# A fused FFT filter and two mixture-of-experts layers on one core: the order of an expert's blocks, prefetch hints for far branches, and the engine that makes the weights' low parts

## The chip, the cores and the metric

One NeuronCore of a Trainium2 chip runs the whole program in one launch. The metric is the device time of one execution in microseconds; lower is better. Engines: PE (TensorE, whose weight loads are listed as PEld), DVE (VectorE), ACT (ScalarE), POOL (GpSimd) and SP (SyncE, which issues most of the DMAs).

## The reference, cut to what matters

```python
X = rfft(x, axis=1)                      # x: (8, 3072, 256)
y = irfft(X * (filt_r + 1j * filt_i))    # a filter per channel
x = y.reshape(24576, 256)
# first layer: every token, 8 experts, top 1
e_idx = argmax(x @ w_gate)
out[e_idx == e] = gate_w * sigmoid(x @ w_output_gate)[e] * (relu(x[e_idx == e] @ w1[e]) @ w2[e])
# second layer: at most 768 tokens an expert, in the order of the tokens; all other rows are 0
```

The number of tokens of an expert is known at run time only, and so is which tokens the second layer takes.

## The kernel before

Products that need more than one pass's precision are split: a high part, rounded by ACT, and a low part, the value less its high part. Each product is then three matmuls (high by high, high by low, low by high). This holds for activations (`xt_h`, `xt_l`, `h_h`, `h_l`) and for the weights (`w_0h`, `w_0l`, ...), whose two sets serve even and odd experts.

**Stages of the profiled execution.** Up to 340 us: the FFT of eight batches and the gate of the first layer, which scatters each token's row into its expert's region of `xs`. The first 86 of 192 token tiles (11008 tokens) are treated first, and what is left is skipped at the end if the second layer's places are full by then (`k.full`, L1864), as they are here. From 340 to 416 us: expert 0's first four blocks in `one_round`, under a guess that they exist (`early`, L712), with the gate's last work beside them. From 416 to 968 us: the rest of the first layer in `Moe.moe1`. Then the second layer in `Moe.moe2`, 24 blocks of 256 rows, until 1307 us.

**An expert in moe1.** Its rows are cut into plain blocks of 256 rows and a last block of 256 (narrow) or 384 rows (wide), which is taken from the end of its region (`cut_blocks`). In program order: block 0, which always runs; then up to seven more plain blocks, each inside the If of the one before it (`nb > j`, L1211), so that an expert with four plain blocks leaves the chain by one far branch over the bodies that are left; then the last block, an If on `wide` with one arm for each size (L911). Here experts 0 to 7 have 4, 5, 5, 4, 4, 5, 5 and 3 plain blocks; experts 3, 4, 5 and 7 have wide last blocks.

**A block (`block1`).** Layer 1 in four pairs (`l1_pair`, 12 matmuls each; ACT makes `h_h` and DVE `h_l`), then `prep` of the next block's rows (four transposes on PE, `xt_h` by ACT, `xt_l` by DVE), then layer 2 for two tiles of 128 rows (24 matmuls each), each followed by an indirect DMA of the rows to `x2tok` on POOL. PE takes all of this in program order. DVE also makes 16 logits of the block before (L1040, a product with a row of `w2gb` and its sum), each block's ending in indirect DMAs to `lgtok`.

**Loads.** SP loads the rows of block j + 1 while block j runs (`load_x`; buffers a0 to a2 for j > 0, b0 and b1 for block 0). Where block j + 1 doesn't exist, `k.ahead` clamps the address to the last real block, and `prep` turns rows that nobody uses. At an expert's start SP loads block 0 of the next expert, block 1 of this one, and the last block's rows (`load_last`). Block 0 turns the rows of block 1 right after its layer 1, and the rows of the last block within its layer 2.

**Weights.** `extra` puts four steps `next_w` into block 0 of each expert: for one quarter of the next expert's weights each, ACT makes the high part, POOL the low part (L810; DVE for the first two experts' weights), and POOL then issues the load of the quarter after next. `moe2` does the same at each expert's block 0.

**Order.** PE, ACT, DVE and SP run in the order in which the program was written; POOL's order is the scheduler's. At the end of an If each engine that skipped its body brings its semaphores up to what the body would have made of them. For POOL's DMA queues that is a wait for the DMAs in flight and then the instruction INC_SWDGE_SEM.

Of the kernel before, what the change touches and what calls it, by code (L numbers as in the profile page):

```python
# [25 lines left out]
EARLY = 4  # L26
# [437 lines left out]
def one_round(k, r, cap):  # L464
# [46 lines left out]
    for bi, b in enumerate(batches):  # L511
# [68 lines left out]
        for q in range(NQ + 2):  # L580
# [17 lines left out]
            if nb is None and q in (4, 6, 8, 10):  # L598
                moe.split_w(0, (q - 4) // 2, nc.vector)
            if nb is None and q == 8 and len(batches) > 1:  # L600
# [4 lines left out]
                with tc.If(early > 0):  # L605
                    moe.load_x(0, 0, True)
        j0, j1 = span[b]
# [54 lines left out]
    def aheads():  # L662
# [21 lines left out]
        )  # L684
        nc.vector.tensor_copy(k.ahead, k.aheadf)

    work = [gate.chain_a2, gate.chain_b, counts, pads, aheads, lambda: cut_blocks(k)]
# [20 lines left out]

    if early is None:
        late()  # L710
    else:
        with tc.If(early > 0) as c:  # L712
            for j in range(1, EARLY):
                moe.load_x(0, j, True)
            weights()
            run(last[0])
            moe.prep(*moe.rows(0, 0))
            moe.head(0, [(0, 1)], last[1:])
            nc.sync.dma_start(out=moe.w2gb, in_=k.a["w2gb"])
            beside = [work[:0], work[:0], work[:2], work[2:4], work[4:5], work[5:]]  # L720
            moe.head(1, [(0, 2)], [lambda f=f: run(*f) for f in beside], True)
            for j in range(2, EARLY - 1):
                moe.head(j, [(0, j + 1)])
            ahead()
            moe.load_x(0, EARLY)
            moe.head(EARLY - 1, [(0, None), (0, EARLY)])
        with c.Else():
            late()
# [5 lines left out]
class Moe:  # L734
# [15 lines left out]
    def alloc(self, p, px):  # L750
# [14 lines left out]
        k.pm = p.tile([128, 3, 8], F32, name="pm")  # L765
# [34 lines left out]
    def split_w(self, g, part, eng=None):  # L800
        nc = self.nc
        eng = eng or nc.gpsimd
        s = g % 2
        if part < 2:
            raw, hi, lo = self.raw1[:, part, :], self.w1[s][0][:, part, :], self.w1[s][1][:, part, :]
        else:
            i = slice(4 * (part - 2), 4 * (part - 2) + 4)
            raw, hi, lo = self.raw2[:, i, :], self.w2[s][0][:, i, :], self.w2[s][1][:, i, :]
        nc.scalar.copy(hi, raw)
        eng.tensor_tensor(out=lo, in0=raw, in1=hi.bitcast(F32), op=ALU.subtract)  # L810
# [63 lines left out]
    def load_x(self, e, j, free=False):  # L874
# [3 lines left out]
        if j > 0 and not free:  # L878
# [4 lines left out]
                max_val=r0,  # L883
# [22 lines left out]
    def last_block(self, e, wide):  # L906
# [3 lines left out]
        nxt = [] if final else [self.rows(e + 1, 0)]  # L910
        with self.tc.If(wide > 0) as c:  # L911
            self.block_wide(s, nxt, final)
        with c.Else():
            xt = [v[:, :, :256] for v in self.xtf]
            self.block1(s, self.xbf[:, :2, :], xt, 3, True, [], nxt, (), final)

    def block_wide(self, s, nxt, final):
# [23 lines left out]
        for rows, x in nxt:  # L941
            self.prep(rows, x)
# [150 lines left out]
    def block1(  # L1093
# [20 lines left out]
        for q in range(4):  # L1114
# [21 lines left out]
        for t in range(2):  # L1136
# [5 lines left out]
            for f in mid[2 + t : 3 + t]:  # L1142
                f()
        for f in side:
            f()
# [17 lines left out]
    def extra(self, e):  # L1163

        n = self.k.last_g
        eng = self.nc.vector if e == 0 else None
        if e + 1 > n:
            return []
        return [lambda q=q: self.next_w(e + 1, n, q, eng) for q in range(4)]
# [8 lines left out]
    def head_late(self, nb, n):  # L1178
# [5 lines left out]
        for j in range(1, n):  # L1184
            with self.tc.If(nb > j):
                self.load_x(0, j + 1)
                self.head(j, [(0, j + 1)])

    def moe1(self, nb0, n0):
# [4 lines left out]
        for e in range(E):  # L1194
# [3 lines left out]
            if e == 1:  # L1198
                nc.sync.dma_start(out=k.iota, in_=k.a["c_iota"])
                nc.sync.dma_start(out=k.jp1, in_=k.a["c_jp1"])  # L1200
            if e == 0:
                nb = nb0
            else:
                nb = nc.values_load(k.plain[0:1, e : e + 1], min_val=0, max_val=nxb)
                self.load_x(e, 1)
# [4 lines left out]
            wide = nc.values_load(k.wide[0:1, e : e + 1], min_val=0, max_val=1)  # L1210
            with ExitStack() as deep:  # L1211
                for j in range(n0 if e == 0 else 1, JU):
                    deep.enter_context(tc.If(nb > j))
                    nxt = []
                    if j + 1 < JU:
                        self.load_x(e, j + 1)
                        nxt = [self.rows(e, j + 1)]
                    self.block1(s, *self.bufs(e, j), 1 + j % 2, True, [], nxt)
# [422 lines left out]
    def moe2(self, n0, n1, plan=None):  # L1641
# [11 lines left out]
        for n in range(n0, n1):  # L1653
# [4 lines left out]
            if b == 0 and e + 1 < E:  # L1658
                mid = [lambda q=q: self.next_w(e + 9, 15, q) for q in range(4)]
# [8 lines left out]
            if b == min(2, nblk - 1):  # L1668
                now, rest = now + rest, []
            for q in range(4):  # L1670
                if n > 0:
                    self.l1_pair(s, self.xt, q)
                if q == 1:
# [16 lines left out]
            for t in range(2):  # L1690
# [18 lines left out]
                go(5 + t)  # L1709
            run(now[split[1] :])  # L1710
# [9 lines left out]
def tile_kernel(ctx: ExitStack, tc, a, out, cap, dbg=None):  # L1720
# [96 lines left out]
    with tc.manual_schedule(engines={ET.PE, ET.Activation, ET.DVE, ET.SP}):  # L1817
        for r in range(len(ROUNDS)):
# [3 lines left out]
            def body():  # L1822
# [4 lines left out]
                with es:  # L1827
                    if last:
                        table(moe.p, r)
                    if last:  # L1830
# [7 lines left out]
                        for q in range(4):  # L1838
                            moe.next_w(8, 9, q)
                        moe.q = es.enter_context(tc.tile_pool(name=f"q{r + 1}", bufs=1))  # L1840
                        moe.go("HPDGKLMBX0123")
                    else:
                        n = len(moe.seq) // E
                        moe.go(LEAD[0])
                        moe.first.close()
                        moe.q = es.enter_context(tc.tile_pool(name=f"q{r + 1}", bufs=1))
                        moe.guess = False
                        pre = nc.values_load(k.known[0:1, 0:1], min_val=0, max_val=1)
                        with tc.If(pre > 0) as c:
                            xg = dict(moe.xg)  # L1850
                            moe.moe2(0, n, BESIDE)
                        with c.Else():
                            moe.xg = xg
                            moe.xg.clear()
                            moe.go(LEAD[1])
                            moe.moe2(0, n)
# [18 lines left out]
LEAD = ("KTUVXLWlMB01ax23yse", "bHPDGeomhctfKLsMBrX0123")  # L1875
# [17 lines left out]
def cut_consts():  # L1893
# [3 lines left out]
    return np.stack([2 * least + 1, 2 * least + 3, least])  # L1897
# [63 lines left out]
```

## Time and profile before

| | |
|---|---|
| median of 3 executions | 1326.87 us (1322.34 to 1327.99) |
| the profiled execution | 1321.05 us, its span 1319.3 us |
| PE busy | 1207.2 us, 92% of the span |
| DVE busy | 872.0 us, 66% |
| POOL busy | 557.2 us, 42% |
| mean granted clock of PE | 0.961 |

The span runs from the first to the last instruction of the profiled execution. A group's idle time names the engine and line whose semaphore ended most of it; "issue" stands for time in which the engine waited for nothing that the profile shows, such as a branch of its own sequencer. An engine's name with a q is its sequencer.

### The profile page before, as it was taken

The numbers are of one execution on the slowest core, as the hardware profiler recorded it, in microseconds if no ns is written. First come the engines' busy times: TensorE is split into PE (matmuls) and PEld (weight loads), VectorE is DVE, ScalarE is ACT, GpSimd is POOL, SyncE is SP. The second block draws the span as 40 slices with busy tenths as digits, with TensorE's granted clock in tenths as the row PEclk, the third lists the DMA queues.
The fourth block names the chain that finished last, engine by engine and source line by source line (L and its number), as shares of the span: only waits on it lengthen the run. The fifth ranks groups of instructions, "written<-read, shape, count | busy, mean of one in ns | idle before, by whom it ended". The sixth has DMA issues, their size and how long they took to land. (4 is left out here: it accounts for less than half of the span.)

```text
span 1319.3 us, 25824 instructions
## 1 busy us (share of the span) xinstructions
PE 1207.2 (92%) x9338; PEld 1172.9 (89%) x9338; DVE 872.0 (66%) x2800; ACT 490.8 (37%) x872; POOL 557.2 (42%) x508
## 2 busy tenths in 40 slices
PE   6999999999885998989998899998997899999996
PEld 6899999989885998889898889988887899999996
DVE  3857676678473875867868688786857755555541
ACT  4363443633421422424233243332323344444431
POOL 0000160446262542634445273452635567676731
PEclk9999999999897999999999899998998999999998
DMA  9343280634563321513224051320512233333210
GB/s 259 123 139 115 63 276 1 204 128 137 185 178 103 108 80 31 165 44 126 70 67 141 27 159 51 117 89 28 157 41 79 66 106 112 97 99 105 71 46 22
DMA packets 85469, 138.95 MB, mean 105 GB/s; under 512 B 13463, under 2 KB 61339, under 8 KB 84889
## 3 DMA queue, kind: packets, MB, share of 16 engines
q1 hardware_dynamic: 61113, 71.07, 17.9%
q0 software_dynamic: 24144, 65.31, 15.5%
q8 instruction: 102, 1.67, 0.5%
q14 instruction: 110, 0.90, 0.2%
HBM read 78.02 MB, written 58.90 MB: 104 GB/s over the span
## 5 line engine op out<-in xcount | busy, mean ns | idle before, releaser
L827 DVE SCALAR_TENSOR_TENSOR h_l<-ps,h_h 128x512 fp32r<-128x512 f32 x252 | 173.4, 689 | 216.0 <-ACT h_h L826 214.4
L1040 DVE SCALAR_TENSOR_TENSOR junk<-x,w2gb 128x256 f32<-128x256 f32 x640 | 283.4, 494 | 0.0
L826 ACT ACTIVATE h_h<-ps 128x512 fp32r<-128x512 f32 x252 | 149.6, 598 | 211.9 <-PE ps L823 202.3
L1020 POOL DMA_INDIRECT lgtok<-lg,wtok x80 | 78.2, 978 | 254.3 <-DVE junk L1040 237.4
L400 POOL DMA_INDIRECT xs<-y,sli x86 | 87.8, 1021 | 214.9 <-DVE tt L234 115.4
L839 PE MATMUL ps<-w_0h,h_l 128*128 128x256 f32 x552 | 160.4, 291 | 17.0 <-DVE h_l L827 16.7
L839 PE MATMUL ps<-w_1h,h_l 128*128 128x256 f32 x552 | 159.9, 290 | 13.2 <-DVE h_l L827 13.1
L837 PE MATMUL ps<-w_0h,h_h 128*128 128x256 f32 x552 | 162.4, 294 | 0.0
L837 PE MATMUL ps<-w_1h,h_h 128*128 128x256 f32 x552 | 161.3, 292 | 0.0
L838 PE MATMUL ps<-w_0l,h_h 128*128 128x256 f32 x552 | 158.4, 287 | 0.0
L838 PE MATMUL ps<-w_1l,h_h 128*128 128x256 f32 x552 | 158.1, 286 | 0.0
L821 PE MATMUL ps<-xt_h,w_0h 128*128 128x256 f32 x480 | 137.4, 286 | 0.7 <-ACT xt_h L871 0.7
L822 PE MATMUL ps<-xt_l,w_0h 128*128 128x256 f32 x480 | 136.4, 284 | 0.2 <-DVE xt_l L872 0.2
L823 PE MATMUL ps<-xt_h,w_0l 128*128 128x256 f32 x480 | 136.3, 284 | 0.0
L821 PE MATMUL ps<-xt_h,w_1h 128*128 128x256 f32 x464 | 128.9, 278 | 1.6 <-ACT xt_h L871 1.6
L822 PE MATMUL ps<-xt_l,w_1h 128*128 128x256 f32 x464 | 128.8, 278 | 0.0
L823 PE MATMUL ps<-xt_h,w_1l 128*128 128x256 f32 x464 | 128.7, 277 | 0.0
L839 PEld LDWEIGHTS ps<-w_0h,h_l 128*128 128x128 f32 x552 | 107.9, 196 | 20.4 <-DVE h_l L827 20.4
L839 PEld LDWEIGHTS ps<-w_1h,h_l 128*128 128x128 f32 x552 | 107.8, 195 | 16.1 <-DVE h_l L827 15.8
L838 PEld LDWEIGHTS ps<-w_0l,h_h 128*128 128x128 f32 x552 | 108.2, 196 | 0.0
L837 PEld LDWEIGHTS ps<-w_0h,h_h 128*128 128x128 f32 x552 | 108.1, 196 | 0.0
L837 PEld LDWEIGHTS ps<-w_1h,h_h 128*128 128x128 f32 x552 | 107.9, 195 | 0.0
(288 smaller groups left out, 3058.1 us busy)
## 6 DMA issues: line engine op xcount, KB each, us to landing
out<-padrow SPq DMA_DIRECT2D x48, 512.0 KB, 6.4
raw<-v POOLq DMA_DIRECT2D x32, 512.0 KB, 4.2
raw<-w POOLq DMA_DIRECT2D x24, 512.0 KB, 4.4
xin<-x SPq DMA_DIRECT2D x40, 240.0 KB, 3.0
xb_a<-xs SPq DMA_DIRECT2D x35, 258.0 KB, 2.9
raw<-w SPq DMA_DIRECT2D x8, 512.0 KB, 5.9
f<-f SPq DMA_DIRECT2D x13, 256.0 KB, 4.6
xs<-padrow SPq DMA_DIRECT2D x8, 387.0 KB, 10.5
```

Source lines behind the costliest of these rows:

```text
L400: i = nc.gpsimd.indirect_dma_start(out=k.xs, out_offset=bass.IndirectOffsetOnAxis(ap=self.sli[:, j : j + 1], axis=0), in_=self.y[:, self.j ...
L821: nc.tensor.matmul(o, lhsT=wh[:, c, sl], rhs=xh[:, c, :], start=c == 0, stop=False)
L822: nc.tensor.matmul(o, lhsT=wh[:, c, sl], rhs=xl[:, c, :], start=False, stop=False)
L823: nc.tensor.matmul(o, lhsT=wl[:, c, sl], rhs=xh[:, c, :], start=False, stop=c == 1)
L826: nc.scalar.activation(hh, ps, AF.Relu)
L827: nc.vector.scalar_tensor_tensor(out=hl, in0=ps, scalar=0.0, in1=hh.bitcast(F32), op0=ALU.max, op1=ALU.subtract)
L837: nc.tensor.matmul(ps, lhsT=hh[:, f, sl], rhs=wh[:, f, :], start=f == 0, stop=False)
L838: nc.tensor.matmul(ps, lhsT=hh[:, f, sl], rhs=wl[:, f, :], start=False, stop=False)
L839: nc.tensor.matmul(ps, lhsT=hl[:, f, sl], rhs=wh[:, f, :], start=False, stop=f == 7)
L1020: i = nc.gpsimd.indirect_dma_start(out=k.lgtok, out_offset=bass.IndirectOffsetOnAxis(ap=tok, axis=0), in_=lg, in_offset=None, bounds_check ...
L1040: self.nc.vector.scalar_tensor_tensor(out=self.junk[:, n % 2, :], in0=x2, scalar=1.0, in1=self.w2gb[:, e, :], op0=ALU.mult, op1=ALU.mult, ...
```

## The change

Five things change.

1. In moe1 the last block of experts 0 to 6 comes directly after block 0 (after the four guessed blocks for expert 0), ahead of the chain of Ifs. Where block j + 1 of an expert doesn't exist, `k.ahead` now gives the start of the next expert's region (`beyond`, `jump`, `k.pend`), so the last plain block turns the rows of the next expert's block 0. The last block no longer does.
2. `mark_branch_hint_location` puts a prefetch hint for a labelled branch into PE's instruction stream, with the value that the branch will have: for `wide` ahead of block 0 (experts 1 to 6), for `nb > j + 1` ahead of block j and in both arms of the last block, for `late`, `known` and `rest`. Expert 0's `wide` gets none.
3. The likely arms of `late` and `known` become the Else arms, so that they end without a branch over the other arm.
4. The weights' low parts are made by DVE everywhere. The step of each quarter is cut in two: the high part in one place, the low part and the load one place later. The places move from the middle of layer 1 to its end, and a fifth comes after layer 2.
5. `cut_blocks` runs before `aheads`, which has four more DVE instructions on 8x8 elements; one more stands in `cut_blocks`.

```diff
+    STT(out=k.pend, in0=k.cntf, scalar=256.0, in1=k.pm[:, 3, :], op0=ALU.mult, op1=ALU.add)
...
+                tc.mark_branch_hint_location("late", 1 - early, [mybir.EngineType.PE])
...
+            in0=k.j256.unsqueeze(1).to_broadcast(b3),
+            in1=k.pend.unsqueeze(2).to_broadcast(b3),
+            op=ALU.is_ge,
...
+        nxt = k.pm[:, 4, :].unsqueeze(2).to_broadcast(b3)
+        nc.vector.tensor_tensor(out=moe.jump, in0=nxt, in1=k.aheadf, op=ALU.subtract)
+        nc.vector.tensor_tensor(out=moe.jump, in0=moe.jump, in1=beyond, op=ALU.mult)
+        nc.vector.tensor_tensor(out=k.aheadf, in0=k.aheadf, in1=moe.jump, op=ALU.add)
...
-    work = [gate.chain_a2, gate.chain_b, counts, pads, aheads, lambda: cut_blocks(k)]
+    work = [gate.chain_a2, gate.chain_b, counts, pads, lambda: cut_blocks(k), aheads]
...
-        with tc.If(early > 0) as c:
...
+        with tc.If(early < 1, label="late") as c:
+            late()
         with c.Else():
-            late()
+            soon()
...
-    def next_w(self, g, n, part, eng=None):
-        self.split_w(g, part, eng)
-        if g + 1 <= n:
-            self.load_w(g + 1, part, self.nc.gpsimd)
+    def next_w(self, g, n):
+        def step(i):
+            if i > 0:
+                self.split_lo(g, i - 1)
+                if g + 1 <= n:
+                    self.load_w(g + 1, i - 1, self.nc.gpsimd)
+            if i < 4:
+                self.split_hi(g, i)
+        return [lambda i=i: step(i) for i in range(5)]
...
+    def split_lo(self, g, part):
+        raw, hi, lo = self.parts(g, part)
+        self.nc.vector.tensor_tensor(out=lo, in0=raw, in1=hi.bitcast(F32), op=ALU.subtract)
...
+    def hint(self, name, value=0):
+        label = f"{name}{self.k.rname}"
+        self.tc.mark_branch_hint_location(label, value, [mybir.EngineType.PE])
+    def more(self, nb, e, j):
+        self.hint(f"n{e}_{j}_", (nb - j + 63) >> 6)
...
-        nxt = [] if final else [self.rows(e + 1, 0)]
-        with self.tc.If(wide > 0) as c:
-            self.block_wide(s, nxt, final)
+        with self.tc.If(wide > 0, label=f"w{e}_{self.k.rname}") as c:
+            tell()
+            self.block_wide(s, final)
         with c.Else():
+            tell()
...
-            if q == 1:
-                for f in mid[:1]:
-                    f()
         for rows, x in nxt[1:] or nxt:
             self.prep(rows, x)
+        for f in mid[:1]:
+            f()
...
+        for f in mid[4:]:
+            f()
...
+                if final:
+                    self.more(nb, e, 1)
+                else:
+                    self.hint(f"w{e}_", wide)
                 self.load_x(e, 1)
                 self.load_last(e)
                 nxt = [self.rows(e, None), self.rows(e, 1)]
                 zero_out(k, ZFFT + (48 - ZFFT) * e // (E - 1))
                 self.block1(s, *self.bufs(e, 0), 0, True, self.extra(e), nxt)
-            wide = nc.values_load(k.wide[0:1, e : e + 1], min_val=0, max_val=1)
+            first = n0 if e == 0 else 1
+            if not final:
+                self.last_block(e, wide, lambda: self.more(nb, e, first))
             with ExitStack() as deep:
-                for j in range(n0 if e == 0 else 1, JU):
-                    deep.enter_context(tc.If(nb > j))
-                    nxt = []
+                for j in range(first, JU):
+                    deep.enter_context(tc.If(nb > j, label=f"n{e}_{j}_{k.rname}"))
                     if j + 1 < JU:
+                        self.more(nb, e, j + 1)
                         self.load_x(e, j + 1)
                         nxt = [self.rows(e, j + 1)]
...
-            if e + 1 == E and self.guess:
-                self.moe2_steps(0)
-            self.last_block(e, wide)
+            if final:
+                if self.guess:
+                    self.moe2_steps(0)
+                self.last_block(e, wide)
...
+                        pre = nc.values_load(k.known[0:1, 0:1], min_val=0, max_val=1)
+                        tc.mark_branch_hint_location("known", 1 - pre, [mybir.EngineType.PE])
+                        moe.go(LEAD[1])
...
-                        with tc.If(pre > 0) as c:
+                        with tc.If(pre < 1, label="known") as c:
...
-                with tc.If(k.fr < 1):
+                with tc.If(k.fr < 1, label="rest"):
```

## Rows read from the trace of the kernel before

**Rows 1.** The page: engines, with busy us, share of the span and instructions.
```profile
PE 1207.2 (92%) x9338; PEld 1172.9 (89%) x9338; DVE 872.0 (66%) x2800; ACT 490.8 (37%) x872; POOL 557.2 (42%) x508
```

**Rows 2.** Windows: start:end, length, busy us and instructions per engine, clock, DMA share, GB/s.
```profile
416.00:968.00 552.00, 495.13 (x3914) 488.47 (x3914) 413.40 (x1556) 181.32 (x323) 247.99 (x217) 0.95 0.29 89
968.00:1052.00 84.00, 70.29 (x514) 67.53 (x514) 55.60 (x162) 26.22 (x59) 40.65 (x35) 0.88 0.22 67
1052.00:1307.00 255.00, 253.13 (x2244) 251.83 (x2241) 130.01 (x393) 110.01 (x208) 156.44 (x126) 1.00 0.27 85
```

**Rows 3.** Waits of PE, 420 to 968 us: who for whom, us in total, times, longest.
```profile
PE ps L821 <- issue: 25.3, 4, 10.2
PE ps L839 <- DVE h_l L827: 22.4, 16, 2.6
```

**Rows 4.** Windows after an exit, after a wait for DVE, and of one plain block.
```profile
510.90:514.30 3.40, 3.36 (x16) 3.39 (x17) 0.17 (x1) 0.30 (x1) 0.00 (x0) 0.51 0.28 82
...
548.70:551.90 3.20, 3.18 (x15) 3.18 (x16) 3.20 (x16) 0.47 (x1) 1.37 (x2) 0.50 0.59 165
...
480.15:491.81 11.66, 11.66 (x103) 11.66 (x102) 9.13 (x40) 3.82 (x7) 3.97 (x5) 1.00 0.27 71
```

**Rows 5.** Timelines (start, us, engine, line), DVE and POOL beside PE, expert 2.
```profile
545.03 2.67 DVE L1040 SCALAR_TENSOR_TENSOR junk<-x,w2gb 128x256 f32<-128x256 f32 x1
...
547.64 0.41 DVE L1040 SCALAR_TENSOR_TENSOR junk<-x,w2gb 128x256 f32<-128x256 f32 x1
...
545.05 2.37 POOL L810 TENSOR_TENSOR w_1l<-raw,w_1h 128x1024 fp32r<-128x1024 f32 x1
...
548.72 0.58 PE L839 MATMUL ps<-w_0h,h_l 128*128 128x256 f32 x1 [2.58 <-DVE h_l L827]
```

**Rows 6.** Line L810, whole span: ns min/median/max, first and last start.
```profile
L810 POOL TENSOR_TENSOR w_0l<-raw,w_0h x28: 2362/2419/2645, 444.1 to 1219.1; 128x1024 fp32r<-128x1024 f32 x28
...
L810 DVE TENSOR_TENSOR w_0l<-raw,w_0h x4: 1224/1224/1300, 325.1 to 334.0; 128x1024 fp32r<-128x1024 f32 x4
```

**Rows 7.** Branch lines, whole span: count, ns min/median/max, first and last start.
```profile
L1211 DVEq COMPARE_BRANCH  x39: 43/47/67, 417.5 to 969.9; - x39
L1211 PEldq COMPARE_BRANCH  x39: 65/70/4252, 418.4 to 969.4; - x39
...
L1211 POOLq INC_SWDGE_SEM  x8: 621/1336/2254, 422.4 to 972.5; - x8
...
L911 PEldq COMPARE_BRANCH  x12: 85/296/3244, 422.8 to 991.7; - x12
...
L712 PEldq COMPARE_BRANCH  x2: 73/1832/3590, 336.0 to 413.8; - x2
...
L1849 PEldq COMPARE_BRANCH  x2: 73/1914/3755, 1003.9 to 1050.1; - x2
```

**Rows 8.** Expert 1's exit, next work of PE and DVE, PE's branch, SP's next load and landing.
```profile
510.94 0.52 PE L821 MATMUL ps<-xt_fh,w_1h 128*128 128x256 f32 x1 [5.18 <-issue]
...
511.52 0.17 DVE L1111 COPY wtok<-ptok 128x2 int32<-128x2 int32 x1 [6.34 <-DMA lgtok<-lg,wtok]
...
L1211 PEldq COMPARE_BRANCH  x2: 192/1844/3497, 503.5 to 507.2; - x2
...
512.11 0.38 SPq L886 DMA_DIRECT2D xb_a<-xs  x1
...
DMA to landing us min/median/max: 2.7/2.7/2.7
```

**Rows 9.** Groups of PE at L865, 416 to 968 us: busy us, mean ns, idle before.
```profile
L865 PE MATMUL ps<-ident,xb_a 128*128 128x128 f32 x124 | 18.6, 272 | 0.0
```

**Rows 10.** Line L1864, the last branch: PE's and POOL's sequencers.
```profile
L1864 PEldq COMPARE_BRANCH  x1: 3797/3797/3797, 1304.8 to 1304.8; - x1
```

**Rows 11.** Waits of PE, 960 to 1060 us.
```profile
PE ps L839 <- DVE h_l L827: 4.0, 2, 3.0
PE ps L1450 <- DVE tg L1338: 4.0, 3, 3.4
```

More of the change, by code (lines that the diff above doesn't have):

```diff
@@ L707, in late, with soon @@
         moe.head_late(nb, EARLY)
+    def soon():
+        for j in range(1, EARLY):
+            moe.load_x(0, j, True)
+        weights()
+        run(last[0])
+        moe.prep(*moe.rows(0, 0))
+        moe.head(0, [(0, 1)], last[1:])
+        nc.sync.dma_start(out=moe.w2gb, in_=k.a["w2gb"])
+        beside = [work[:0], work[:0], work[:2], work[2:4], work[4:5], work[5:]]
+        moe.head(1, [(0, 2)], [lambda f=f: run(*f) for f in beside], True)
+        for j in range(2, EARLY - 1):
+            moe.head(j, [(0, j + 1)])
+        ahead()
+        moe.load_x(0, EARLY)
+        moe.head(EARLY - 1, [(0, None), (0, EARLY)])
     if early is None:
@@ L711, in one_round @@
     else:
-        with tc.If(early > 0) as c:
[L713 to L726, printed above, removed]
+        with tc.If(early < 1, label="late") as c:
+            late()
         with c.Else():
-            late()
+            soon()
     np = nc.values_load(k.plain[0:1, 0:1], min_val=0, max_val=k.R // 256)
@@ L764, in alloc @@
         )
-        k.pm = p.tile([128, 3, 8], F32, name="pm")
+        k.pm = p.tile([128, 5, 8], F32, name="pm")
+        k.pend = p.tile([128, 8], F32, name="pend")
+        self.beyond, self.jump = (p.tile([128, 8, 8], F32, name=n) for n in ("beyond", "jump"))
         nc.sync.dma_start(out=k.pm, in_=k.a["c_pm"])
@@ L792, in load_w, with parts, split_hi, split_w @@
             )
[L794 to L802 removed]
+    def next_w(self, g, n):
[7 more added lines that the diff above has]
+        return [lambda i=i: step(i) for i in range(5)]
+    def parts(self, g, part):
         s = g % 2
         if part < 2:
[L805 to L810, printed above, removed]
+            return [t[:, part, :] for t in (self.raw1, *self.w1[s])]
+        i = slice(4 * (part - 2), 4 * (part - 2) + 4)
+        return [t[:, i, :] for t in (self.raw2, *self.w2[s])]
+    def split_hi(self, g, part):
+        raw, hi, _ = self.parts(g, part)
+        self.nc.scalar.copy(hi, raw)
+    def split_lo(self, g, part):
+        raw, hi, lo = self.parts(g, part)
+        self.nc.vector.tensor_tensor(out=lo, in0=raw, in1=hi.bitcast(F32), op=ALU.subtract)
+    def split_w(self, g, part):
+        self.split_hi(g, part)
+        self.split_lo(g, part)
     def l1_pair(self, s, xt, q):
@@ L1165, in extra @@
         n = self.k.last_g
[L1166 to L1169, printed above, removed]
+        return self.next_w(e + 1, n) if e + 1 <= n else []
     def head(self, j, nxt, side=(), pe_tail=False):
@@ L1187, in head_late @@
                 self.head(j, [(0, j + 1)])
+        self.load_x(0, n)
+        self.prep(*self.rows(0, n))
     def moe1(self, nb0, n0):
@@ L1658, in moe2 @@
             if b == 0 and e + 1 < E:
-                mid = [lambda q=q: self.next_w(e + 9, 15, q) for q in range(4)]
+                mid = self.next_w(e + 9, 15)
                 if not plan:
@@ L1669, in moe2 @@
                 now, rest = now + rest, []
+            if self.k.rname == "r0" and n + 1 == len(seq):
+                full = nc.values_load(
+                    k.full[0:1, 0:1], engines=(mybir.EngineType.PE,), min_val=0, max_val=1
+                )
+                self.tc.mark_branch_hint_location("rest", 1 - full, [mybir.EngineType.PE])
             for q in range(4):
@@ L1709, in moe2 @@
                 go(5 + t)
+            run(mid[4:])
             run(now[split[1] :])
@@ L1837, in body @@
                             moe.load_w(8, q)
-                        for q in range(4):
-                            moe.next_w(8, 9, q)
+                        for f in moe.next_w(8, 9):
+                            f()
                         moe.q = es.enter_context(tc.tile_pool(name=f"q{r + 1}", bufs=1))
@@ L1896, in cut_consts @@
     least = np.array([EARLY] + [1] * (E - 1))
-    return np.stack([2 * least + 1, 2 * least + 3, least])
+    far = np.where(np.arange(E) == E - 1, 2.0**20, 0.0)
+    nxt = rows_per_expert() * np.minimum(np.arange(E) + 1, E - 1)
+    return np.stack([2 * least + 1, 2 * least + 3, least, far, nxt])
 def misc_consts(cap):
```

37 lines of the change are left out of this document (23 added, 14 removed).

## Prediction

> **What bounds the kernel now.** I read the page first: PE is busy for 92% of the span, DVE for 66% [rows 1]. So time is won where PE stands still or runs at a lower clock, and the windows by stage say where. In the second layer from 1052 us on PE is busy for 253.1 of 255.0 us at full clock: nothing is to be had there but matmuls [rows 2]. In the first layer (416 to 968 us) PE is idle for 552.0 - 495.1 = 56.9 us and its mean clock is 0.95 [rows 2]. The list of PE's waits in that stage splits the idle time: 25.3 us in 4 waits for nothing but its own sequencer, at the exits into a narrow last block; 22.4 us in 16 waits for `h_l` of DVE [rows 3]; the other 9 us stand at the exits into wide blocks.
>
> The clock adds to both. [...]
>
> **Why PE waits for DVE.** The timelines of both engines beside POOL's show it. A logit's product takes DVE 0.41 us, but one that meets POOL's low part took 2.67 us and ended with POOL's 2.37 us instruction; `h_l` stands behind it, and PE waited 2.58 us for it [rows 5]. The kernel has 56 such low parts on POOL, 2.4 us each; DVE makes one in 1.22 us [rows 6].
>
> **Low parts on DVE.** Removed in the first layer: the 22.4 us, and, at an estimate for six of the seven experts, 1.6 us of slow clock, 10 us: 32 us. Added on DVE per expert: 4 x 1.22 = 4.9 us; removed there: each of four POOL instructions can hold a DVE instruction for up to 2.3 us (2.67 - 0.41), so DVE comes out about even. DVE is busy for 9.1 of a plain block's 11.66 us [rows 4], 2.5 us short of PE. In block 0 it now needs 9.1 + 4.9 = 14.0 us and a little for the last block's rows, against some 13 us of PE. What is late next is thus the `h_l` of the block behind block 0: PE needs the first of them 5.5 us after that block's start, so the lag of 1 to 2 us is mostly covered. Without that cover each expert would pay the lag. I charge 0.6 us an expert, 4 us in all; bounds 0 and 30 us (a rival, below). Net: -28 us. POOL loses nothing by its place: its loads of the next weights wait for DVE instead of itself, and have an expert's length to land.
>
> **Exits of the chain.** PE's far branches took up to 4.25 us (3.50 at expert 1's exit) [rows 7, 8]. PE's sequencer runs ahead: that branch began at 503.5 us, 2.3 us before the last matmul ended (510.94 - 5.18 = 505.76) [rows 8]. A hinted branch that takes what a fall-through takes (0.07 us [rows 7]) would end before PE runs dry. But another wait starts at the same point. POOL closes the skipped bodies' semaphores only when its DMAs have landed, with an INC_SWDGE_SEM of 0.6 to 2.3 us [rows 7]; DVE's next copy came 5.8 us after PE's last matmul, and SP's load of the next expert's block 1 (buffer a1, whose earlier readers are in the chain) was issued at 512.11, 6.35 us after it, to land 2.7 us later: 9.05 us [rows 8]. Before, the last block lay between the exit and block 0, and hid that. Now block 0 follows at once. Its layer 1 is half of a block's matmuls: a block less its four transposes (0.6 us: 124 transposes in 18.6 us [rows 9]) is 11.06, half is 5.5 us. Then PE wants block 1's rows: it is idle for 9.05 - 5.5 = 3.6 us an exit, however fast the branch. With 1.7 to 3 us of slow clock behind it an exit costs 5.3 to 6.6 us, say 5.9; experts 0 to 6 make 41 us. SP's load of the last block's rows is queued behind that load and lands after it; PE wants them one layer 2 tile later, so I price it at 0 (its cover is that tile, some 2.8 us). Before, these exits cost 56.9 - 22.4 = 34.5 us of idle time and some 12 us of clock (seven exits at 1.7), 46 us.
>
> **Entries.** Expert 0's arm of `late` ended with a branch of 3.59 us and went on into two more [rows 7]; the three made the 10.2 us wait [rows 3]. Now only the unhinted one over the wide arm is left (at most 3.2 us [rows 7], less 2.3 of run-ahead), with some slow clock and a wait of DVE behind it: 4 us. Exits and entry after: 45 us. Net: -1 us.
>
> **Transposes.** For experts 0 to 6 four transposes turned rows that nobody used, and the last block turned the next expert's: one of the two goes, 7 x 0.6 = -4 us, on PE's path.
>
> **Expert 7, `known`, `rest`.** Expert 7's exit keeps its place, so the hint helps it: -1 us of its share. `known` jumps over the other arm in 3.76 us [rows 7]; less the 2.3 us of run-ahead, -1 us. The last branch (`rest`) takes 3.8 us from 1304.8 us [rows 10] but POOL's end of the DMAs comes later: 0; bounds 0 and -1 us.
>
> **Start of the second layer.** PE waits there 4.0 us for `h_l` and 4.0 us for the gates' casts [rows 11], with a clock of 0.88 over the stage [rows 2]; both stand behind POOL's low parts. DVE gets four low parts of 1.22 us in the same stretch, which take back about 5 us. -4 us; bounds 0 and -10 us.
>
> **At nothing.** The hints' register arithmetic on PE hides in the 2.3 us of run-ahead, at exits in the 3.6 us wait; the five new DVE instructions on 8x8 elements are nearest to the 0.17 us copy [rows 8], some 1 us once, under the load wait of that stretch; loads that now carry the next expert's rows are as many as before.
>
> **The sum.** -28 - 1 - 4 - 2 - 4 = -39 us, against the profiled execution's 1321.05: 1282. The median of the three runs lies 5.8 us above that execution, so I forecast 1287 us as the median.
>
> **Rivals.**
> 1. *The load is not held back* (15%): if SP's load after the exit need not wait for POOL's increments, an exit costs one to two us and little clock, 2.8 instead of 5.9: 7 x 3.1 = 22 us better, 1265 us. For it: the hints would then pay in full. Against it: buffer a1 is read only by bodies in the chain, and SP's load waited at that point at the exit shown [rows 8].
> 2. *DVE becomes the bound* (14%): block 0's DVE work, started late by POOL's increments (its copy came 5.8 us after the exit [rows 8]), pushes `h_l` past PE's need by 2.5 us, and the slow clock adds 1.6: 7 x 4.1 = 29 us, 1316 us. It decides once DVE's lag passes PE's 5.5 us of layer 1. Against it: 2.5 us of DVE slack in each later block [rows 4].
> 3. *The hints do nothing* (10%): the change would not do what it says at far branches. The exits' branches, at 3.5 us less 2.3, end before the load does, so only the three narrow entries of experts 1, 2 and 6 (3.2 - 2.3 = 0.9 us and 1.7 of clock each) and `known` pay: 8 us, 1295 us. [...]
> 4. *A hint pushes out the code that comes next* (6%): slower. In the first layer 23 of the 39 branches (39 less two for each of 8 exits) are the not-taken ones of bodies that run, at 0.07 us now [rows 7]. If a hint's fetch displaced the fall-through code, each would pay about 3.5 - 2.3 = 1.2 us and 1.7 us of clock: 23 x 2.9 = 67 us, 1354 us. It turns the gain into a loss from 39 / 23 = 1.7 us a branch. Against it: the hint carries the branch's true value.
>
> **How the numbers follow.** The forecast's own case has 55%, from 1274 to 1302 us. The range of 8 in 10 reaches to rival 1 below and near rival 2 above: 1264 to 1314 us. The measurement can tell about 0.5% of this kernel from no change, 6.6 us. Faster by more: the forecast, rivals 1 and 3 and most of rival 2, 0.87. Within: the rest of rival 2 and some of rival 4's weaker forms, 0.07. Slower: rival 4, 0.06.
>
> **What would show it.** No DVE product of the logits over 1 us, and PE's waits for `h_l` in the first layer at 5 us or less instead of 22: the low parts. PE's branches of the chain under 0.3 us: the hints. PE's transposes waiting for `xb_a` some 3 us, seven times, with SP's load 6 us after the exit: the exits. 28 transposes less at L865 in the stage: the transposes. The forecast is wrong if exits are free of that wait, if `h_l` stays late behind DVE's low parts, or if bodies that run begin with a fetch.

## The result, and the profile after

The changed kernel takes 1265.7 us (median of 4 runs, 1258.9 to 1268.1) beside 1326.1 us for the kernel before (1322.3 to 1328.0): a ratio of 0.954, 95% interval 0.950 to 0.958. The forecast was 1287 us, the range 1264 to 1314: the sign and the range held, but the gain is 60 us where 39 were forecast. The profiled execution took 1263.8 us, its span 1262.0; before, 1321.05 and 1319.3.

The page of the changed kernel (engines with busy us, share and instructions; then TensorE's granted clock in 40 slices), and its windows by stage, which answer [rows 1, 2]:

```profile
PE 1187.2 (94%) x9310; PEld 1154.3 (91%) x9310; DVE 860.4 (68%) x2854; ACT 489.3 (39%) x865; POOL 419.0 (33%) x452
...
PEclk9999999999999999999999999999978999999998
```
```profile
416.00:914.00 498.00, 473.69 (x3915) 468.00 (x3913) 393.98 (x1582) 181.89 (x320) 181.85 (x189) 1.00 0.31 98
914.00:996.00 82.00, 72.31 (x514) 69.36 (x514) 50.91 (x171) 25.99 (x60) 30.24 (x32) 0.85 0.24 74
996.00:1250.00 254.00, 252.71 (x2240) 251.82 (x2240) 143.01 (x412) 108.94 (x207) 95.59 (x102) 1.00 0.26 85
```

The first layer's stage shrank from 552 to 498 us; the start of the second layer gained 2 us, the rest 1. The stage's granted clock is 1.00 where it was 0.95 [rows 2]. PE's waits in it (us, times, longest) answer [rows 3]:

```profile
PE ps L898 <- DMA xb_a<-xs: 10.9, 7, 2.8
PE ps L854 <- ACTq L1261: 8.0, 6, 1.4
PE ps L854 <- issue: 2.3, 1, 2.3
PE ps L854 <- ACT x L1180: 1.2, 1, 1.2
PE ps L872 <- DVE h_l L860: 0.9, 3, 0.3
```

The 22.4 us for `h_l` are 0.9, the 25.3 us for the sequencer 2.3. In their place stand a wait of 1.1 to 2.3 us at each exit, mostly for ScalarE's sequencer (8.0 us in six waits), which takes its own branch at L1261 (38 and 50 ns at expert 2), and one for block 1's rows. Expert 2's exit (start, us, engine, line), then the window behind its second wait (PE, PEld, DVE, ACT, POOL busy, granted clock):

```profile
580.27 0.28 PE L872 MATMUL ps<-w_0h,h_l 128*128 128x256 f32 x1
581.95 0.38 PE L854 MATMUL ps<-xt_h,w_1h 128*128 128x256 f32 x1 [1.41 <-ACTq L1261]
```
```profile
587.70 0.37 SPq L919 DMA_DIRECT2D xb_a<-xs  x1
```
```profile
590.57 0.66 PE L898 MATMUL ps<-ident,xb_a 128*128 128x128 f32 x4 [2.77 <-DMA xb_a<-xs]
```
```profile
590.60:594.00 3.40, 3.40 (x29) 3.40 (x30) 2.07 (x10) 2.48 (x3) 0.42 (x1) 1.00 0.98 302
```

PE's last matmul ends at 580.55, SP issues the load 7.15 us later and PE gets the rows 2.8 us after that, as forecast (6.35 and 2.7). Until then SP had waited for the DMAs to `x2tok` that read that buffer (us, times, longest):

```profile
SPq L919 <- DMA x2tok<-x,xb_a: 21.4, 1, 21.4
```

But two waits of PE, of 1.4 and 2.8 us, with half a block of work between them stand where the forecast had one of 3.6, and in this profile no lower clock follows.

VectorE's products of the logits, for [rows 5] (ns min/median/max; none reaches 0.5 us):

```profile
L1081 DVE SCALAR_TENSOR_TENSOR junk<-x,w2gb x640: 404/416/493, 390.5 to 912.5; 128x256 f32<-128x256 f32 x160
```

The branches and transposes, for [rows 7, 10] and [rows 9] (L952 chooses the wide or narrow last block, L1261 ends the bodies, L1912 is `known`; first of the kernel after, then the next-expert rows of the kernel before):

```profile
L1261 PEldq COMPARE_BRANCH  x39: 65/70/1463, 428.5 to 913.8; - x39
...
L952 PEldq COMPARE_BRANCH  x12: 65/308/3112, 418.1 to 939.6; - x12
...
L1912 PEldq COMPARE_BRANCH  x1: 374/374/374, 951.6 to 951.6; - x1
...
L898 PE MATMUL ps<-ident,xb_a 128*128 128x128 f32 x124 | 19.0, 275 | 10.9 <-DMA xb_a<-xs 10.9
```
```profile
L865 PE MATMUL ps<-ident,xb_b 128*128 128x128 f32 x28 | 4.2, 272 | 0.0
```

Those 28 transposes are the ones that went: 9338 matmuls became 9310.

### The profile page after: what moved, and what is told of

The parts are those of the page before. It is cut to its first block, busy times and chain, and to the rows that moved or that the text cites. A ratio compares the mean times of both kernels' runs of the same rounds, so it can differ in the third digit from the quotient of the medians.

```text
span 1262.0 us, 25769 instructions
## 1 busy us (share of the span) xinstructions
PE 1187.2 (94%) x9310; PEld 1154.3 (91%) x9310; DVE 860.4 (68%) x2854; ACT 489.3 (39%) x865; POOL 419.0 (33%) x452
## 5 line engine op out<-in xcount | busy, mean ns | idle before, releaser
L1081 DVE SCALAR_TENSOR_TENSOR junk<-x,w2gb 128x256 f32<-128x256 f32 x640 | 235.5, 420 | 0.0
L872 PE MATMUL ps<-w_1h,h_l 128*128 128x256 f32 x552 | 156.4, 283 | 0.6 <-DVE h_l L860 0.6
L871 PEld LDWEIGHTS ps<-w_1l,h_h 128*128 128x128 f32 x552 | 105.8, 192 | 0.0
```

The lines of the kernel that those rows point to most:

```text
L871: nc.tensor.matmul(ps, lhsT=hh[:, f, sl], rhs=wl[:, f, :], start=False, stop=False)
L872: nc.tensor.matmul(ps, lhsT=hl[:, f, sl], rhs=wh[:, f, :], start=False, stop=f == 7)
L1081: self.nc.vector.scalar_tensor_tensor(out=self.junk[:, n % 2, :], in0=x2, scalar=1.0, in1=self.w2gb[:, e, :], op0=ALU.mult, op1=ALU.mult, ...
```

## The experiments

Twelve runs follow, of nine kernels, on three chips. On one chip the kernel before takes 1390.7 us (last section); the table has the runs of the others: the first layer's stage of each profile, from the start of PE's branch at the end of the head to the start of its exit branch at expert 7. Idle is the stage less the union of PE's matmuls and weight loads; "half clock" is half of PE's busy time inside stretches at a granted clock of 0.50. Both are worked out from the traces.

| kernel | median us | before, beside it | stage us | idle | half clock |
|---|---|---|---|---|---|
| before | 1326.1 | | 552.0 | 56.7 | 22.4 |
| low parts on VectorE only (b_lo) | 1292.7 | 1324.6 | 522.3 | 37.3 | 14.5 |
| hints only (b_hints) | 1310.7 | 1324.6 | 538.2 | 45.7 | 19.8 |
| low parts and hints (b_lo_hints_2) | 1271.6 | 1323.7 | 505.3 | 26.8 | 7.9 |
| all but VectorE (a_lo_pool) | 1312.8 | 1324.6 | 535.9 | 48.9 | 15.1 |
| all but the hints (a_no_hints) | 1269.8 | 1324.6 | 497.8 | 24.6 | 4.9 |
| all: the changed kernel | 1265.7 | 1326.1 | 493.3 | 23.8 | 0.0 |
| the same again (after_2) | 1264.0 | 1323.7 | 495.8 | 23.6 | 3.4 |
| all, rows loaded twice (a_delay_2) | 1286.4 | 1323.7 | 520.0 | 38.6 | 16.1 |
| all, rows in own buffers (a_free_2) | 1253.2 | 1323.7 | 481.9 | 13.4 | 0.0 |

### One part alone: VectorE's low parts

```
-        eng.tensor_tensor(out=lo, in0=raw, in1=hi.bitcast(F32), op=ALU.subtract)
+        self.nc.vector.tensor_tensor(out=lo, in0=raw, in1=hi.bitcast(F32), op=ALU.subtract)
```
with the five new places in the block, and nothing else of the change.

> The kernel before with one part of the change: VectorE makes the low parts, at the new places; the blocks' order, the branches and the hints stay as before. Before stands at 1326. Theory A (two leaks that add up: the waits on h_l while GpSimd and VectorE share work, and the exits): the h_l waits between 420 and 968 us fall from 22.4 us to about 1, the half-clock stretches that followed six of the seven 2.6 us waits (3.4 us each, worth 1.7 us each) go, some 4 us of transposes' and copies' waits go, and the exits keep their 24 us and their own half-clock stretches: 1326 - 21 - 10 = about 1293 to 1297. Rival B (the clock falls only where both leaks come close together, so that it returns only once both are gone): only the waits go, 1303 to 1307, with eight or more half-clock stretches left in that stage. Rival C (VectorE becomes the bound of block 0, as the prediction's second rival had it): the waits return in block 0 under another releaser and the time is 1310 or more.

Measured: 1292.7 us, ratio 0.977 (0.971 to 0.982), 31.9 us less. Theory A. The waits:

```profile
PE ps L835 <- issue: 14.8, 3, 5.1
PE ps L835 <- DVE wtok L1125: 10.5, 1, 10.5
PE ps L943 <- issue: 5.4, 2, 4.9
PE ps L853 <- DVE h_l L841: 2.2, 7, 0.3
```

The `h_l` waits fell from 22.4 to 2.2 us, so VectorE did not become the bound (rival 2, theory C). What remains are the exits and expert 0's entry (10.5), and in or just behind each of these waits a half-clock stretch begins, also where the wait was 1.9 to 2.2 us.

### One part alone: the hints

```
-        deep.enter_context(tc.If(nb > j))
+        deep.enter_context(tc.If(nb > j, label=f"n{e}_{j}_{k.rname}"))
...
+        self.more(nb, e, j + 1)          # a hint ahead of each body
```

> The kernel before with one part of the change: the chain's and the last block's branches have a label, and a body names the coming exit ahead of time; order of blocks and GpSimd's low parts stay as before. Theory A (the hint itself takes the jump's 3.4 us off TensorE's queue): the exit jump falls to about 0.4 us; the exits of experts 1, 2 and 6, which make a second far jump of 2.7 to 3.2 us, go from 5 us of idle time to about 1.5 if the second jump can still start ahead of TensorE's drain, the others from 1.8 to 1.3: 3 x 3.5 + 3 x 0.5 = 12 us, and half of the 27 us of half-clock stretches behind exits goes with it at most (13 us): 1301 to 1315. Rival B (the exits are held by what is not the jump, by the other engines' catch-up and the load's landing): the jump falls to 0.4 us, idle time stays within 4 us of before, and the time is 1321 to 1326. Rival C (a hint as good as nothing in this kernel): the jump keeps its 3.4 us, 1324 to 1328.

Measured: 1310.7 us, ratio 0.990 (0.984 to 0.995), 13.9 us less: theory A. The jump at expert 1's exit fell from 3497 ns to 373 and PE's gap there from 5.2 to 1.9 us; at expert 2 the second jump, over the wide arm, still took 3.0 us right behind the first and the gap stayed at 4.6:

```profile
509.02 0.36 PE L821 MATMUL ps<-xt_fh,w_1h 128*128 128x256 f32 x1 [1.93 <-DVEq L1221]
...
591.83 0.55 PE L821 MATMUL ps<-xt_fh,w_0h 128*128 128x256 f32 x1 [4.57 <-issue]
```

Not every hinted jump became short: those at the exits of experts 3 and 5 took 2.0 and 1.6 us.

### One part undone: GpSimd's low parts

```
-        self.nc.vector.tensor_tensor(out=lo, ...)
+        eng = self.nc.vector if g < 2 else self.nc.gpsimd
+        eng.tensor_tensor(out=lo, ...)
```

> The changed kernel with one part undone: GpSimd makes the low parts again (at the changed kernel's places, one step after the high parts), order and hints as changed. Changed stands at 1266. Theory A (two leaks that add up): GpSimd's 2.4 us operations meet VectorE's 0.4 us logit products in seven blocks, each product beside one takes 2.7 us, seven waits on h_l of about 2.6 us come back (18 us) and a half-clock stretch behind most of them (7 x 1.7 = 12 us): 1290 to 1300. Rival B (the waits come back but the clock holds, since the exits no longer take their share): 1280 to 1287 and at most two half-clock stretches between 420 and 914 us. Rival C (at the new places GpSimd's work falls into VectorE's pauses): under 6 us, 1266 to 1272.

Measured: 1312.8 us, 47.1 us more than the changed kernel, past theory A's upper end. Its waits, then DVE and POOL in expert 2's last block:

```profile
PE ps L873 <- DVE h_l L861: 16.2, 9, 3.7
...
PE ps L873 <- DVE h_l L978: 7.6, 10, 2.2
...
PE ps L856 <- DVE xt_fl L892: 2.2, 2, 1.1
...
PE ps L974 <- DVE xt_fl L892: 2.0, 2, 1.1
```
```profile
538.22 3.77 DVE L1082 SCALAR_TENSOR_TENSOR junk<-x,w2gb 128x256 f32<-128x256 f32 x1
```
```profile
539.34 2.36 POOL L840 TENSOR_TENSOR w_1l<-raw,w_1h 128x1024 fp32r<-128x1024 f32 x1
```

At the new places GpSimd's work also meets the last block's copies: 28.0 us of waits where the old places had 22.4, one product held for 3.77 us, and 15.1 us of half clock where the changed kernel has none. With low parts on GpSimd the new order gains nothing (1312.8 against 1310.7 with hints alone).

### One part undone: the hints

```
     def hint(self, name, value=0):
         label = f"{name}{self.k.rname}"
-        self.tc.mark_branch_hint_location(label, value, [mybir.EngineType.PE])
+        return
```

> The changed kernel without the hints ahead of the chain's and the last block's branches (those of the other far branches stay); order and VectorE's low parts as changed. Changed stands at 1266. Theory A (the jump's 3.4 us starts 2.3 us before TensorE drains, and what follows it in the changed kernel, ScalarE's branch and its semaphore, takes 1.3 us of the same time): about +0.4 us at each of seven exits and +1.2 us at the entries of the two narrow last blocks whose hint took effect, and the clock holds: 1269 to 1273. Rival B (the clock falls behind the longer gaps as it did before the change): as A and some 8 to 16 us of half-clock stretches' cost more, 1278 to 1290. Rival C (the hints do nothing, the prediction's third rival): 1264 to 1268, with jumps of 0.4 us all the same.

Measured: 1269.8 us, ratio 0.960 (0.954 to 0.966), 4.1 us over the changed kernel's first median: theory A's size, though not all of its terms. The intervals of the two ratios overlap, so 4 us is not clear of noise. PE's branches and waits:

```profile
L1261 PEldq COMPARE_BRANCH  x39: 65/70/3814, 429.3 to 920.4; - x39
...
L952 PEldq COMPARE_BRANCH  x12: 65/302/602, 418.9 to 941.0; - x12
```
```profile
PE ps L854 <- issue: 15.9, 6, 3.0
PE ps L898 <- DMA xb_a<-xs: 4.4, 5, 1.4
PE ps L854 <- PEq L1261: 2.4, 1, 2.4
```

The exits' jumps take 3.4 to 3.8 us again and the exits' own waits 18.3 us instead of 10.3; but the rows land meanwhile, and their wait falls from 10.9 to 4.4. Idle time differs by 0.8 us, half clock by 4.9, or by 1.5 beside the second profile of the changed kernel. So what the hints bring in the new order is small, and that it is mostly clock is not shown. The narrow entries, which I had priced at 1.2 us each, take 0.35 to 0.6 us without a hint.

### Low parts and hints in the old order

Both edits above on the kernel before. It ran on two chips, first on the one on which the kernel before takes 1390.7 us (last section).

> The kernel before with two parts of the change, VectorE's low parts and the hints; the last block still ends the chain. VectorE alone gave 1293, the hints alone took 14 us off 1325, the whole change stands at 1266. Theory A (the hints' gain does not hang on the low parts): 1293 - 14 = 1276 to 1282, and what is left to 1266, some 13 us, is the new place of the last block: the exits of experts 0 and 2 keep gaps of 4 us and more, from a second far jump right behind the first, with a half-clock stretch each. Rival B (the hints' gain needs the new order, since the second jump stands right behind the first): 1288 to 1293. Rival C (order does nothing by itself): 1264 to 1269.

> VectorE's low parts and the hints in the old order, again, now beside the changed kernel; its ratio to before was 0.9727 the last time. Theory A (what is left to the changed kernel is the order, and it is the second far jump behind the first at experts 0 and 2 and the clock behind it): 12 to 25 us over the changed kernel. Rival B (order is worth nothing): within 4 us of it.

Measured: 1353.1 of 1390.7 us, then 1271.6 of 1323.7 us beside 1264.0 for the changed kernel. The hints' gain does not hang on the new order: 21 us behind b_lo, more than the 14 alone. The two overlap instead. With VectorE's low parts the hints alone take 21 us off b_lo, the new order alone, with its swapped arms, 23 (a_no_hints, 1269.8), and both together 27 to 29: either removes most of what the far jumps cost. Beside the hints the order is thus worth 7.6 us between the medians, in the gap between the two theories, and the intervals of the two ratios (0.956 to 0.965 and 0.950 to 0.961) overlap. Of these 4.2 us are the transposes, the rest lies in

```profile
PE ps L835 <- issue: 18.0, 3, 11.2
```

that is above all expert 0's entry (11.2 us, three branches of 3.7, 5.0 and 3.3 us in a row) and expert 2's exit (4.9 us: branches of 0.3, 1.1 and 0.2 us, and then 3.1 us in which PE's sequencer waits for nothing that the trace shows), less the wait for rows that only the new order has.

### The order alone

The changed kernel with GpSimd's low parts and without the hints.

> The kernel before with the new order and what it brings along (rows of the next expert read ahead, swapped arms), with GpSimd's low parts and without the hints of the chains. With hints it stood at 1313. Theory A (the order is worth 13 us or more by itself, but at its places GpSimd's low parts cost 47 us where they cost 32 at the old ones, so that the two nearly cancel): 1313 + 4 to 8 for the hints = 1316 to 1321, that is 4 to 9 us under before. Rival B (the hints are worth 14 us here as they were in the old order): 1324 to 1330. Rival C (the parts add up): 1325 - 13 = 1309 to 1313.

Measured, on the slower chip: 1387.6 of 1390.7 us, ratio 0.999 (0.997 to 1.001). Taken as it is, that lies between A (4 to 9 us under before) and B (up to 5 over). But the three kernels that ran on both chips have higher ratios on this one: 0.973 against 0.960, 0.957 against 0.947, 0.978 against 0.971. With 0.006 to 0.012 off, an estimate, this kernel would take 1307 to 1315 us beside 1325, around theory C (1309 to 1313) and just under A. So this run settles none of the three, and what the order is worth with GpSimd's low parts stays open.

### The wait made longer

```
                 self.load_x(e, 1)
+                self.load_x(e, 1)
```
The second load writes the same buffer; it was put in so that block 1's rows land one landing later.

> The changed kernel with block 1's rows loaded twice at each later expert's entry, the second load behind the first, which puts the wait for them off by one landing, 2.0 to 2.7 us, at seven places. Changed stands at 1266, its waits for these rows are 0.5 to 2.8 us and no half-clock stretch follows any. Theory A (the clock falls behind a single wait of TensorE of some length, whatever the wait is for): the waits grow to 2.5 to 5.5 us, that is +14 to +19 us, and half-clock stretches come back behind most of them, +1.7 to +3.4 us each: 1290 to 1305. [...] Rival C (the second load goes by beside the first): 1264 to 1268.

> Block 1's rows loaded twice, again, now beside the changed kernel; the last time its seven waits for these rows were 2.1 to 5.5 us, 25.7 us in all, and half-clock stretches stood behind them. Theory A (a single longer wait is enough for the clock to fall): the waits cost 14 to 19 us over the changed kernel's and the clock 6 to 16 us more, 20 to 35 us over it in all, and half-clock stretches stand behind most waits of over 3 us. Rival B (the clock falls on the slower chip alone): 14 to 19 us over the changed kernel and at most two such stretches in the first layer's stage.

Measured: 1358.5 of 1390.7 us, then 1286.4 us, 22.4 us over the changed kernel beside it. Theory A, at the lower end of its time. The wait, and windows behind three of them:

```profile
PE ps L898 <- DMA xb_a<-xs: 27.7, 7, 5.1
```
```profile
599.10:602.50 3.40, 3.40 (x16) 3.40 (x17) 1.63 (x6) 2.25 (x3) 0.00 (x0) 0.50 0.93 291
440.60:444.00 3.40, 3.40 (x16) 3.40 (x17) 1.65 (x8) 2.27 (x3) 0.00 (x0) 0.50 0.98 297
519.20:522.60 3.40, 3.40 (x16) 3.40 (x17) 1.61 (x6) 2.23 (x3) 0.00 (x0) 0.50 0.96 291
```

The waits grew by 16.6 us (27.7 against 11.1), 2.4 each, and the half clock's cost by 12.7 us. Six of the seven waits were 3.5 to 5.1 us long, and in or just behind each of the six a half-clock stretch of 3.4 or 6.8 us begins (a seventh stretch stands behind an exit's own wait of 1.4 us). In the changed kernel's two profiles the same waits are 0.5 to 2.8 us: behind 14 of them there are two such stretches, after 2.8 and 1.9 us, both in the second profile.

### The wait taken away

```
+        if j == 1 and e > 0:
+            return self.xb[f"c{e % 2}"], self.xt      # two buffers more
...
             if 0 < e < E - 1:
                 self.load_x(e + 1, 0)
+                self.load_x(e + 1, 1)
-                self.load_x(e, 1)
```

> The changed kernel with block 1's rows of every later expert in two buffers of their own, loaded one expert ahead beside its block 0's rows, so that this load no longer waits for a chain's body to give its buffer back. The changed kernel stands at 1266 and waits 10.9 us in seven places for those rows. Theory A (that load is what now ends last after the exits): the waits go, exits keep their 1.1 to 2.3 us, 1254 to 1258, and the first-layer stage falls from 493 to about 482 us. Rival B (another wait stands right behind it, the narrow rows' copies or the last block's landing): 1261 to 1266. Rival C (the earlier loads collide with the head's or with GpSimd's weight loads): 1268 or more.

> Block 1's rows in buffers of their own, loaded one expert ahead, again, now beside the changed kernel. The last time its seven waits for these rows were gone, the exits cost 1.4 to 2.5 us, and its ratio to before was 0.9567. Theory A (the load was what ended last): 8 to 11 us under the changed kernel of the same call. Rival B (the exits' catch-up takes the place: what came in while TensorE waited for the rows now comes in while it waits for ScalarE): 0 to 4 us under it. Rival C (the earlier loads collide in the head): over it.

Measured: 1331.4 of 1390.7 us on the slower chip, where no changed kernel ran beside it, then 1253.2 us beside 1264.0: 10.7 us less, ratio to before 0.947 (0.942 to 0.952). Theory A. Its waits in the stage begin with

```profile
PE ps L855 <- ACTq L1264: 8.1, 6, 1.5
PE ps L855 <- issue: 2.1, 1, 2.1
PE ps L873 <- DVE h_l L861: 1.2, 4, 0.3
```

and none is for `xb_a`; the exits' own waits stay as they were and nothing took the place. The load that was held back by the chain's buffer is thus what ended last, and this version beats both kernels.

### The changed kernel beside them

> The changed kernel again, beside the next three, since the chip of the last four kernels ran the kernel before in 1391 us, 5% over the 1325 us of the others, with 1 us gaps of TensorE in straight code that nothing in the trace releases. On a chip like the first: 1262 to 1269 beside 1322 to 1328, ratio 0.954. On one like the second: theory A (the slower chip adds the same to both kernels, ahead of the changed stage): 1326 to 1332 beside 1391, ratio 0.954 to 0.958. Rival B (it adds more to the kernel with more far jumps, so the change is worth more there): under 1322.

Measured: 1264.0 us, ratio 0.956 (0.950 to 0.961), on a chip like the first. How the change fares on the other was not run; the three variants that ran on both took 72 to 82 us more there, the kernel before 67.

## Why the prediction was right, and where it was short

**Low parts, forecast -28.** Right: alone -31.9 us. Of [rows 3] 20 us of waits went and 8 us of half clock (estimate: 10, at six times half of the 3.2 us that [rows 4] has at a granted clock of 0.50). The charge of 0.6 us an expert for VectorE's lag, 4 us in all, was too high: in the changed kernel 0.9 us of waits for `h_l` are left. The contention is as read from [rows 5, 6]: the logits' products average 420 ns instead of 494 on the page, and 2.4 us operations on POOL are gone. Its worth is not one number, though: undone in the new order, at the new places, it costs 47 us.

**Exits and entry, forecast -1.** This is the step that failed, by 22 to 24 us. From b_lo to the changed kernel the time falls by 27.0 us, of which 4.2 are transposes. The forecast had 45 us left after the change: 7 x 5.9 at the exits and 4 at expert 0's entry. Measured: the seven exits idle for 21.2 us (10.3 at the exit itself, 10.9 at the rows), 3.0 each against 3.6 forecast; expert 0's entry has no gap (its unhinted branch took 347 ns, forecast up to 3.2 us); and the half clock behind them, forecast at 1.7 to 3 us each or 16 us (1.7 is half of the 3.4 us at 0.51 in [rows 4], 3 was my estimate), is 0.0 and 3.4 us in the two profiles. 45 - 21 = 24.

So the mechanism of the exit was right (a buffer that comes free late, SP's load 7.15 us after the drain, 2.8 us to land), the idle time nearly so, and the clock term mis-sized. I took the clock's fall from the kernel before, where a stretch stands behind six of the exits of experts 0 to 6, and expected one wait of 3.6 us. But PE waits at the exit itself, at six of the seven for ScalarE's branch (up to 1.4 us), and the load runs on under that: the same time comes as a wait of 1.5 and one of 1.6 us on average, with half a block between (581.95 to 587.80 us at expert 2).

a_delay_2 bears the term out for longer waits: the clock fell at six of six of 3.5 us and more, and its 16.1 us of half clock are 2.3 for each of seven exits, as forecast; but there, too, an exit's own wait stands ahead. Behind single waits of 1.7 to 3.0 us the clock fell at all three such exits of b_lo, at three of seven of a_no_hints and at two places of after_2. Over the ten profiles of the table I counted PE's waits in the stage, and how many of them have a half-clock stretch that begins in the wait or within 2 us behind it: one of 67 waits of 0.5 to 1.6 us, 28 of 50 of 1.7 to 3.0, all 22 of 3.5 and more. The changed kernel's two profiles have three and five waits in the middle group and none in the last. That the split saved the clock is thus supported by many waits, though no run changes the split alone, and what decides in the middle group stays open.

**The sum, and luck.** The terms add up to 1287.9, not 1287. That the time fell inside the range is in part luck: it lies 1.7 us above the lower end, and that end had been set by rival 1, whose condition did not come true.

**Transposes, forecast -4.** Right: 28 of them, 4.2 us.

**Expert 7 and `known`, forecast -2.** The exit's gap is 1.9 us before and 2.0 after, each ended by DVE's sequencer in its own exit (L1211, now L1261); the jump of 3755 ns at the end of the arm of `known` is gone, one of 374 ns stands ahead of the arm, and where a gap of 1.6 us stood behind the old jump there are two of 0.7 for `xt_h` and `xt_l`. About nothing came.

**Second layer, forecast -4.** About half came: the stage went from 84 to 82 us [rows 2]; the waits of [rows 11] fell, a 2.9 us wait for `tot` and a 2.3 us one for gathered rows took part of it back.

**The head.** It is 4 us longer in the changed profile (75.8 to 80.1 us, from 338 us to its last branch). The kernel with hints alone, whose head is the one before, took 79.6, and the other kernels of the table 77.6 to 83.3: as far as this shows it is scatter, not the change's.

**The rivals.** The time is rival 1's (1265), but not by its mechanism: the load *is* held back, and only a_free, which frees it, shows what rival 1 would give: 1253. Rival 2 is out (0.9 us for `h_l`). Rival 3: the hints do work, the exits' jumps of 3.4 us and more became 0.34 to 0.37 (1.46 at expert 6's exit), and still they are worth only some 4 us in the new order, not clear of noise, since the load's wait stands behind the jump (10.9 us, 4.4 without the hints).

Without a hint the exits' jumps take PE 3.4 to 4.3 us in the kernel before and 3.4 to 3.8 in a_no_hints, and DVE at most 0.07 in both. An exit skips at least three plain blocks, of some 205 instructions of PE and PEld and some 40 of DVE each [rows 4]. What makes the jumps long on PE and short on DVE was not shown.

Rival 4: bodies that run (24 branches, not 23: expert 0's exit has only one) still pay 65 to 78 ns. Something like rival 4 shows in one place: at expert 6's narrow entry the hinted branch took 3112 ns (a gap of 1.2 us), 2128 in after_2 and 548 in a_free_2, and 367 without a hint in a_no_hints; why is open. The three narrow entries take 0.35 to 3.1 us with a hint and 0.35 to 0.6 without, so these hints brought nothing that shows.

## What to carry to other kernels

Price the clock by the length of single waits, not by their sum, as far as these runs show: two short waits with work between them cost little more than themselves here, while waits lengthened to 3.5 us and more cost 1.35 times what was added (22.4 us for 16.6). When a jump is made cheap, look for the load that was issued behind it; here the hints won some 4 us, not clear of noise, and the load's own buffer 11. When two remedies aim at the same wait, run each alone: hints and order each took over 20 us off, and together 27 to 29. GpSimd instructions that hold up VectorE's have no fixed price: at other places, in another order of blocks, the same 56 low parts cost 47 us instead of 32.

## What the runs showed of the hardware

One of the chips ran the kernel before in 1390.7 us instead of 1324. The same instructions have the same durations there (in a_free on both chips a median of 416 and 418 ns for a logit's product, within 1% for PE's groups), but PE stands still in straight code, in waits of up to 2.2 us that nothing in the trace releases, and PE's granted clock from 160 to 310 us is 0.83 in a_free there, where the changed kernel's on the first chip is 1.00. Waits of PE from 160 to 310 us in a_free on that chip, and in the same kernel on the other:

```profile
PE ps L147 <- issue: 13.2, 16, 1.7
PE ps L243 <- issue: 12.3, 11, 1.7
PE ps L225 <- issue: 8.2, 6, 2.2
```
```profile
PE ps L213 <- POOL yf L197: 1.8, 1, 1.8
```

The lines are those of the FFT ahead of the changed stage. What holds PE's instructions back there was not tried.

A jump over the same wide arm, without a hint, took 0.35 to 0.6 us where PE reaches it in straight flow (a_no_hints), 2.7 to 3.2 us at all eight places of the kernel before and b_lo where it stands right behind a far jump; with the last block behind block 0 that cost was gone here without any hint.
